# Gated mix of dilated attention and a spatial MLP: the v gathers move to the GpSimd queue, the gate rows move behind the first score gather, and four PSUM banks swap roles

## The chip, the cores and the metric

The kernel runs on one core of a Trainium2 chip. The metric is the device time of one execution in microseconds (us). Four runs of the kernel before the change took 651.54, 651.75, 653.66 and 653.85 us; their median is 652.71 us. The run that was profiled is the one of 653.85 us.

## What is computed

The reference mixes two branches of one input `x` (2048 tokens, 1024 features) with a gate per token:

```python
g = sigmoid((x * gate_w).sum(-1, keepdims=True))
# branch A: attention, 32 heads of 32, each token sees itself and 7 earlier ones, 2 apart
q, k, v = split(x @ wqkv)
idx = pos[:, None] - 2 * arange(8)[None, :]          # masked where negative
o = softmax(q . k[idx] / sqrt(32)) @ v[idx]
a = o @ wo
# branch B: gated MLP over tokens
z = gelu(x @ w_in)                                    # 3584 wide, halves z1 and z2
b = (z1 * (w_sp @ layernorm(z2) + b_sp)) @ w_out
return g * a + (1 - g) * b
```

## The kernel before the change

The matrix products run on TensorE, nearly all of them as Strassen-like quads of seven block products (`strassen`, `chain`), issued by `product` (L402). Each quad owns four PSUM banks. `bank_roles` holds two sets of four banks (banks 0 to 3, banks 4 to 7), and each quad takes one set in the roles X, Y, Z, V and writes back the order in which the next quad takes it (L411 to L413 in `strassen`; the v quads are called with `turn=False` and keep it). Inside a quad VectorE adds the shared product to a bank (`plus`, L473) and ScalarE copies or evacuates banks (L420 to L492, L869). The next block product of the same bank waits for these.

Attention works in eight groups of four heads. For one group g:

- `qk_quad` or `qk_tile` makes q and k.
- `band_blocks` makes three sets of score blocks on banks 4 to 7 (32x64 tiles, L355). ScalarE evacuates each set (L363, 1.8 us for a full one). Two stores per set write it to the DRAM buffer `band_d[g]`. For group 0 there are four such sets (`first_bands`).
- `load_bands` gathers `band_d[g]` into `att_L` by two DMAs, one for each half of the tokens. Each run that they read is `W*HG` = 32 half-precision numbers, 64 bytes.
- VectorE takes maxima and subtracts them (L639 to L642), ScalarE takes the exponential (L630), VectorE makes weights (L651 to L660; L655 multiplies by the gate row `g_att`).
- `load_v` gathers v rows from the DRAM buffer `v_d` into one of two SBUF slots: 128 partitions with a run of `NJJ*C` = 3840 bf16 numbers (7680 bytes) each, 960 KB.
- VectorE multiplies weights and v and adds up (L676, L680, L681, L685; 1.22 us for a product of 2048 columns). Per group this is 18.4 us of VectorE work.

v of groups 0 to 2 is written to `v_d` early, by twelve stores of 128 KB from GpSimd (L310). v of groups 3 to 7 comes later from eight quads (`v_quad`), evacuated by L589 and L595 and stored by SyncE.

The gate is one small product (L995), a tanh (L996), and two scalings into `g_s` and `omg_h` (L997, L998). Two stores write them to the DRAM rows `g_d` and `og_d`; a gather of 8 KB brings `g_d` back as `g_att`, in the layout of attention.

The order of work is written out by a planner inside the kernel. It keeps a clock for TensorE, ScalarE, VectorE, SyncE and the DMA engines. `due` holds transfers with the time from which they may be issued; `advance` issues them, and picks VectorE's attention steps, in the order of their planned times. `settle` pins every instruction of these engines behind the one before it, so that the engines run exactly that order. This begins at `live[0] = True`, just behind the gate. `T_START` sets three planner times at that point: when the score stores of group 0 have landed, when the score banks are free, and when the v stores have landed. GpSimd is not in the planner and not pinned: its instructions run in program order as soon as their semaphores allow.

Every plain DMA from `live[0] = True` on goes through SyncE (shown as L189, a helper line), so it stands in one queue behind all earlier ones. In the order before the change, SyncE issues: the last score stores of group 0, the two gate rows, the two score gathers of group 0, the gather of `g_att`, the v gather of group 0, the v and q/k weights, the v gather of group 1.

While group g = 2 (and g = 4) is worked on, `among_bands` issues the seven products of one quad and puts a score set behind some of them: behind products 1, 3 and 6, but for g = 2 behind 1, 3 and 5. Then the eight v quads follow, the first one alone for two products (X and V), then a pair of marker products on banks 5 and 6 (`mark`, L558), then two quads at a time.

Of the kernel before, what the change touches and what calls it, by code (L numbers as in the profile page):

```python
# [13 lines left out]
P = 128  # L14
S = 2048
# [6 lines left out]
C = HG * DH  # L22
W = 8
NJ = 16
NJJ = NJ + 14
# [33 lines left out]
def kernel(  # L59
# [13 lines left out]
    nc = tc.nc  # L73
# [16 lines left out]
    v_d = dpool.tile([NG, S + 16, C], BF, name="v_d")  # L90
# [3 lines left out]
    g_d = dpool.tile([S], F32, name="g_d")  # L94
    og_d = dpool.tile([S], F16, name="og_d")
# [3 lines left out]
    g_s = sm.tile([16, P], F32, name="g_s")  # L99
# [5 lines left out]
    omg_h = sm.tile([16, P], F16, name="omg_h")  # L105
    g_att = sm.tile([P, NJ], F32, name="g_att")
# [91 lines left out]
    sync = _SyncProxy()  # L198
# [3 lines left out]
    clock = dict(PE=0.0, ACT=0.0, DVE=0.0, SP=0.0, DMA=0.0)  # L202
    live = [False]
    pinned = {}
# [52 lines left out]
    def dma(ready, dur, f, landed=None, timed=False):  # L257
        if not live[0]:
            return f()
        item = [ready, dur, f, landed, timed]  # L260
        due.append(item)
        return item
# [64 lines left out]
    for i in range(4):  # L327
        vp_tile(i, middle=None)
    band_at = [0]
    last_sub = [None]  # L330
    last_evac = [None]
    BAND_SETS = [(0, 8, 2), (1, 1, 7), (9, 1, 7)]

# [1 line left out]
    stored = {}  # L335

    def band_blocks(g, first, step, n, pairs=None):
        qt, kt_ = qT_slots[g % 2], kT_slots[g % 2]
        if first == 0:
            st = band0  # L340
        else:
            st = band_slots[band_at[0] % 3]
            band_at[0] += 1
        for item in stored.get(id(st), ()):
            issue(item)
        ready = pe(T_BAND * (0.3 if n < 3 else 1.0), band_free[0])
        lo = W - 1 if first == 0 else 0
        for m in range(n):
            e, b = divmod(first + m * step, 8) if pairs is None else (m // pairs, first + m % pairs)
            for q in range(2):  # L350
                skip = lo if q == 0 else 0
                at = P * b + QB * q
                for h in range(HG):
                    hp = slice(DH * h, DH * (h + 1))
                    nc.tensor.matmul(banks[4 + h][QB * q:QB * (q + 1), m * KW + skip:(m + 1) * KW], qt[hp, e, at:at + QB],  # L355
                                     kt_[hp, e, at - (W - 1) + skip:at + QB], start=True, stop=True,
                                     tile_position=(DH * h, QB * q), skip_group_check=True)
        band_free[0] = act(0.55 if n < 3 else 1.73, ready + 0.2) + 0.15
        if lo:
            nc.scalar.copy(st[QB:P, 0:n, 0:lo, :], _sub_ap(psum_all[QB:P, :], 4 * 512, [[KW, n], [1, lo], [512, HG]]))  # L360
        dst = st[:, 0:n, lo:KW, :]
        src = _sub_ap(psum_all, 4 * 512 + lo, [[KW, n], [1, KW - lo], [512, HG]])
        nc.scalar.copy(dst, src)  # L363
        bd = band_d[g]

        def landed(t):
            band_data[g] = max(band_data[g], t)

        stored[id(st)] = []
        for q in range(2):  # L370
            for e in range(1 if pairs is None else 2):
                k = n if pairs is None else pairs
                dst = bass.AP(tensor=bd.tensor, offset=bd.offset + (2 * first + 16 * e + q) * BS, ap=[[BR, QB], [2 * step * BS, k], [1, BR]])
                src = st[QB * q:QB * (q + 1), e * k:(e + 1) * k].rearrange("p m k h -> p m (k h)")
                stored[id(st)].append(dma(band_free[0], 0.1 * k, lambda dst=dst, src=src: sync.dma_start(dst, src), landed))

    def band_set(g, x):
        band_blocks(g, *BAND_SETS[x])
# [12 lines left out]
    bank_roles = [banks[0:4], banks[4:8]]  # L391
# [4 lines left out]
    last_store = [None]  # L396
# [170 lines left out]
    def v_quad(i):  # L567
        st = vst_slots[i % 4]
        vs = vq_slots[i % 2]

        def parts(m, a, *bs):
            d = st[:, a, :].rearrange("p (g d h) -> p g d h", g=GR, h=HG)
            full = slice(3 * m, 3 * m + 2)
            at, half, hs = (0, 256, slice(0, 2)) if m == 0 else (64, 0, slice(2, 4))
            yield [d[:, full]] + [b[:, at:at + 256].rearrange("p (g h d) -> p g d h", g=2, h=HG) for b in bs]
            yield [d[:, 2, :, hs]] + [b[:, half:half + 64].rearrange("p (h d) -> p d h", h=2) for b in bs]

        for item in stored.get(id(st), ()):
            issue(item)
        stored[id(st)] = []  # L580

        def store(a):
            dv = bass.AP(tensor=v_d.tensor, offset=v_d.offset + (GP * (S + 16) + 16 + (i + 8 * a) * P) * C, ap=[[C, P], [(S + 16) * C, GR], [1, C]])
            stored[id(st)].append(dma(max(clock["ACT"], clock["DVE"]), 0.92, lambda: sync.dma_start(dv, st[:, a, :].rearrange("p (g c) -> p g c", g=GR)), v_landed))

        def put(m, a, b):
            act(0.85, clock["PE"] + 0.2)
            for dst, src in parts(m, a, b):
                nc.scalar.copy(dst, src)  # L589
            if m:  # L590
                store(a)

        def put_sum(m, a, b):
            dve(0.75, clock["PE"] + 0.2)
            insts = [nc.vector.tensor_tensor(dst, src, v, ALU.add) for dst, src, v in parts(m, a, b, vs)]  # L595
            if not m:
                store(a)
            return insts[0]

        return strassen([wvr[0][:, k, :] for k in K4], [wvr[0][:, 4 + k, :] for k in K4], [wvr[1][:, 4 + k, :] for k in K4],  # L600
                        *[[wvs[q][:, k, :] for k in K4] for q in range(4)], *x_tiles(i), vs,
                        lambda X: put(0, 0, X), lambda Z: put_sum(0, 1, Z), lambda V: put(1, 0, V), lambda Y: put_sum(1, 1, Y),
                        N=VH, flip=True, turn=False)

    def load_v(g):
        v_t = v_slots_t[g % 2]
        sync.dma_start(v_t, bass.AP(tensor=v_d.tensor, offset=v_d.offset + (g * (S + 16) + 2) * C, ap=[[NJ * C, P], [1, NJJ * C]]))


    FR, LATE, WZ_LATE = 0.4, 0.5, 4.0  # L610
# [215 lines left out]
    SQH = 8  # L826
    squares = [(n, x) for n in range(16) for x in range(2)]
    LEAN = (True, True)
    T_START = (0.0, 0.0, 0.0)

    def square(n, x, junk):
        c = slice(x * HF, (x + 1) * HF)
# [48 lines left out]
    BAND_AT = (1, 3, 6)  # L881

    def among_bands(g, quad):
        x = 0
        for n in range(7):
            next(quad)
            step()
            if n + 1 in (BAND_AT if g != 2 else (1, 3, 5)):
                band_set(g, x)
                x += 1  # L890
                step()
        bands_have[0] = g + 1
        next(quad, 0)
# [101 lines left out]
    gate_mm = nc.tensor.matmul(glT, gl_s[:], ident32[:], start=True, stop=True)  # L995
    gate_act = nc.scalar.activation(omg[:], glT, ACT.Tanh, scale=0.5)  # L996
    nc.vector.tensor_scalar(g_s[:], omg[:], 0.5, 0.5, ALU.mult, ALU.add)  # L997
    gate_vec = nc.vector.tensor_scalar(omg_h[:], omg[:], -0.5, 0.5, ALU.mult, ALU.add)  # L998
    sync.dma_start(bass.AP(tensor=g_d.tensor, offset=g_d.offset, ap=[[P, 16], [1, P]]), g_s[:])
    gate_dma = sync.dma_start(bass.AP(tensor=og_d.tensor, offset=og_d.offset, ap=[[P, 16], [1, P]]), omg_h[:])  # L1000

    settle()
    live[0] = True
    for inst in (gate_mm, gate_act, gate_vec, gate_dma):
        pinned[inst.ins.engine] = inst.ins.name
    for x in clock:
        clock[x] = 0.0
    band_data[0], band_free[0], v_data[0] = T_START
    clock["SP"], clock["DMA"] = 0.5, 1.5
    stored.clear()  # L1010
    bands_have[0] = 1
    next_bands()
    dma(0.0, 0.1, lambda: sync.dma_start(g_att[:], bass.AP(tensor=g_d.tensor, offset=g_d.offset, ap=[[NJ, P], [1, NJ]])))
    next_v(1)
    def load_wvr():
        for m in range(2):
# [8 lines left out]
    for g in range(NG):  # L1025
        main = with_quads(g, group_tiles(g))
        if g in (1, 2, 3, 4):
            load_wqk_later(g + 3, clock["PE"])
        hold[0] = g == NG - 1
        paired = play_group(g)  # L1030
        if not paired:
            play(main[0:8 - (not g)])
        if g == 2:
            first = v_quad(0)
            for _ in range(2):
                next(first)
                step()
            mark(bank_roles[1][1:3], VH)
            run(v_quad(1), first, step=step)
            for i in range(2, 8, 2):  # L1040
                run(v_quad(i), v_quad(i + 1), step=step)
            advance(clock["PE"] + 1.0)
            v_have[0] = NG
            next_v()
            load_later(0, clock["PE"] + 4.0, 6.0)
        if not paired:
            play(main[8 - (not g):])
# [559 lines left out]
            load_act(fp // 2 - 1)  # L1607
    out_sums_late()
    traced[0] = len(nc.cur_bb.bb.instructions)
    pinned[gate_dma.ins.engine] = last_store[0].ins.name  # L1610
    for xa in ((1, 1), (0, 1), (0, 0), (1, 0)):
        load_block(1, *xa)
    act_sums(0)
# [46 lines left out]
```

## Time and profile before

| What | Value |
|---|---|
| Median of four runs | 652.71 us (651.54 to 653.85) |
| The profiled execution | 653.85 us, its span from first to last instruction 652.1 us |
| TensorE (PE) busy | 638.5 us, 98% |
| VectorE (DVE) busy | 519.5 us, 80% |
| ScalarE (ACT) busy | 297.3 us, 46% |
| GpSimd (POOL) busy | 15.4 us, 27 instructions |
| Granted TensorE clock | 1.00 |
| The SyncE queue (q1) | 95.70 MB, 61.6% of the time of 16 DMA engines |
| The GpSimd queue (q0) | 1.57 MB, 0.9% |
| A v gather, 960 KB (8 of them, SyncE) | median 6.8 us from issue to landing |
| A score gather, 64 KB (16) | median 3.4 us |
| A full score store, 248.5 KB (28) | median 4.7 us |
| A v store from GpSimd, 128 KB (12) | median 4.3 us; 0.75 us of GpSimd each |
| The gate rows, 8 KB and 4 KB; `g_att`, 8 KB | 2.7, 2.5 and 2.7 us |

How to read the views: every row of a timeline is a start in us from the first instruction, a length, the engine, the line of the code, the operation, what it writes and reads, and a count. A bracket at the end tells how long the engine stood idle before it, and what ended that wait. SPq rows are DMA issues; the transfer itself follows. In a table of stretches the last two columns are the busy share of the DMA engines and what they moved.

### The profile page before, as it was taken

Reading aid. Unit: us, or ns where it says so; the run is one execution under the profiler, and the core shown is the slowest. Engines: PE = TensorE matmul, PEld = TensorE weight load, DVE = VectorE, ACT = ScalarE, POOL = GpSimd, SP = SyncE. Lnnn points to the kernel's source line nnn. Section 1 sums busy time; section 2 is a strip of 40 time slices with the busy share of each in tenths; the row PEclk is TensorE's granted clock in tenths of the full one; section 3 lists DMA queues with packets and bytes.
Section 4 is the critical chain, followed back from the end, with each engine's and each line's share of the span. In section 5 each row is a group of like instructions: output and inputs, shape, how many; then the busy total and the mean of one; then the engine's idle time right before and its main releaser. Section 6 shows DMA issues by size and latency. Waiting matters only on the chain.

```text
span 652.1 us, 11298 instructions
## 1 busy us (share of the span) xinstructions
PE 638.5 (98%) x4345; PEld 336.7 (52%) x4391; DVE 519.5 (80%) x816; ACT 297.3 (46%) x644; POOL 15.4 (2%) x27
## 2 busy tenths in 40 slices
PE   8999999999989999999999999999999999999997
PEld 4544467444445555444444444444444444868684
DVE  0357988998799999999988766987659999696852
ACT  3557677676667777799644112111121112202120
POOL 2210000000000000001000000000000000000000
PEclk9999999999999999999999999999999999999999
DMA  9979564787778103248985567569587385655411
GB/s 205 193 179 278 119 145 109 171 211 178 160 182 218 22 11 115 64 130 219 267 224 193 120 163 176 125 178 276 114 188 169 93 148 96 121 138 126 117 34 48
DMA packets 227173, 98.18 MB, mean 151 GB/s; under 512 B 174496, under 2 KB 214064, under 8 KB 227120
## 3 DMA queue, kind: packets, MB, share of 16 engines
q1 hardware_dynamic: 226256, 95.70, 61.6%
q0 software_dynamic: 576, 1.57, 0.9%
q8 instruction: 34, 0.56, 0.4%
q14 instruction: 19, 0.16, 0.1%
q10 hardware_dynamic: 288, 0.20, 0.1%
HBM read 44.31 MB, written 36.61 MB: 124 GB/s over the span
## 4 chain that ended last, share of the span: by engine, by line
PE 85%; DVE 4%; ACT 4%; DMA 3%; SPq 2%; issue 1%; DVEq 0%
PE psum_all L402 69%; PE psum_all L1484 8%; PE psum_all L293 4%; DMA band_d<-arena 2%; PE psum_all L303 2%; ACT arena L838 1%; PE psum_all L355 1%; SPq L189 1%; DVE arena L676 1%; ACT arena L1175 1%; DVE psum_all L473 1%; DVE arena L680 1%; DMA arena<-in_A_wqkv_dram 1%; SPq L178 1%; DVE arena L545 0%
## 5 line engine op out<-in xcount | busy, mean ns | idle before, releaser
L402 PE MATMUL psum_all<-arena 128*128 128x512 f16 (+6 forms) x2481 | 502.8, 362 | 6.2 <-DVE psum_all L473 2.7
L402 PEld LDWEIGHTS <-arena 128*128 128x128 f16 (+1 forms) x2518 | 245.1, 98 | 256.4 <-issue 6.6
L676 DVE TENSOR_TENSOR arena<-arena,att_A 128x2048 f16<-128x2048 bf16 x64 | 75.4, 1219 | 0.3
L473 DVE TENSOR_TENSOR psum_all<-psum_all,arena 128x512 f32<-128x512 f32 (+1 forms) x78 | 51.0, 669 | 8.1 <-PE psum_all L402 5.0
L1484 PE MATMUL psum_all<-arena 128*128 128x256 f16 (+1 forms) x468 | 51.7, 273 | 0.0
L1484 PEld LDWEIGHTS <-arena 128*128 128x128 f16 x468 | 45.8, 98 | 5.7
L783 ACT ACTIVATE arena<-psum_all 128x448 bf16<-128x448 f32 x64 | 34.2, 545 | 20.8 <-DVE psum_all L473 10.1
L293 PE MATMUL psum_all<-arena 128*128 128x512 bf16 x183 | 42.0, 379 | 1.3 <-issue 0.6
L420 ACT COPY psum_all<-psum_all 128x512 f32<-128x512 f32 (+1 forms) x24 | 12.5, 520 | 66.1 <-PE psum_all L402 65.4
L1175 ACT ACTIVATE arena<-psum_all 128x512 bf16<-128x512 f32 x56 | 31.2, 615 | 20.8 <-PE psum_all L402 12.9
L680 DVE TENSOR_TENSOR arena<-arena 128x2048 f16<-128x2048 f16 x32 | 37.9, 1217 | 0.0
L363 ACT CAST arena<-psum_all 128x1988 f16<-128x1988 f32 (+3 forms) x25 | 34.0, 1359 | 2.8 <-PE psum_all L355 2.3
L838 ACT ACTIVATE arena<-arena 128x896 bf16<-128x896 bf16 x32 | 30.9, 980 | 0.0
L545 DVE TENSOR_TENSOR arena<-arena 128x512 f16<-128x512 bf16 (+5 forms) x60 | 30.1, 534 | 0.4
L444 ACT COPY psum_all<-psum_all 128x512 f32<-128x512 f32 (+1 forms) x24 | 12.3, 518 | 37.5 <-PE psum_all L402 36.8
L293 PEld LDWEIGHTS <-arena 128*128 128x128 bf16 x192 | 18.1, 98 | 21.6 <-DMA arena<-in_A_wqkv_dram 0.7
L869 ACT CAST arena<-psum_all 128x512 bf16<-128x512 f32 x40 | 22.2, 591 | 12.2 <-DVE psum_all L473 9.9
L388 DVE TENSOR_TENSOR arena<-arena 128x2048 f16<-128x2048 bf16 x8 | 9.4, 1221 | 22.2 <-ACT gl_s L306 21.0
L426 ACT COPY arena<-psum_all 128x512 f32<-128x512 f32 (+1 forms) x24 | 12.7, 533 | 26.4 <-PE psum_all L402 23.3
L486 ACT COPY psum_all<-psum_all 128x512 f32<-128x512 f32 (+1 forms) x39 | 21.7, 574 | 6.1 <-PE psum_all L402 5.5
L431 ACT COPY psum_all<-psum_all 128x512 f32<-128x512 f32 (+1 forms) x24 | 12.4, 516 | 25.6 <-PE psum_all L402 24.8
L549 DVE TENSOR_TENSOR arena<-arena 128x1024 f16<-128x1024 f16 (+1 forms) x16 | 11.3, 713 | 15.7 <-PE psum_all L402 15.7
(113 smaller groups left out, 531.2 us busy)
## 6 DMA issues: line engine op xcount, KB each, us to landing
arena<-v_d SPq DMA_DIRECT2D x8, 960.0 KB, 6.8
z_d<-arena SPq DMA_DIRECT2D x14, 512.0 KB, 3.8
arena<-z_d SPq DMA_DIRECT2D x14, 512.0 KB, 4.3
zg_d<-arena SPq DMA_DIRECT2D x56, 128.0 KB, 2.2
arena<-zg_d SPq DMA_DIRECT2D x32, 224.0 KB, 3.5
band_d<-arena SPq DMA_DIRECT2D x28, 248.5 KB, 4.7
arena<-in_A_wqkv_dram SPq DMA_DIRECT2D x16, 256.0 KB, 4.5
o_d<-arena SPq DMA_DIRECT2D x4, 1024.0 KB, 6.2
```

The costliest lines, as they stand in the source:

```text
L293: nc.tensor.matmul(ps[:], w[:, t, kt, :], xT[:, kt, 512 * c:512 * (c + 1)], start=(kt == 0), stop=(kt == KT - 1))
L363: nc.scalar.copy(dst, src)
L402: nc.tensor.matmul(bank[:, 0:N], lhsT, rhs, start=(start and m == 0), stop=(m == n - 1), skip_group_check=True)
L473: last_add[0] = nc.vector.tensor_tensor(out[:, n], a[:, n], vs, ALU.add)
L545: return [lambda a=a: nc.vector.tensor_tensor(*a) for a in args]
L676: lambda ws=ws, in0=in0, in1=in1: tt(p5[:, ws], in0[:, ws], in1[:, ws], ALU.mult)), False
L680: lambda a=p3[:, ws], b=p3[:, ws.start + 4:ws.stop + 4]: tt(a, a, b, ALU.add)), not n
L783: nc.scalar.activation(z2[:, i + 8 * a, ZC * c:ZC * (c + 1)], bank[:, 0:ZC], ACT.Gelu_apprx_tanh, accum_out=s1[:, 4 * n + c:4 * n + c + 1])
L838: return nc.scalar.activation(junk, src, ACT.Square, accum_out=(s2, s2h)[x][:, n:n + 1])
L869: nc.scalar.copy((qT_slots, kT_slots)[t][g % 2][:, :, 256 * (c + 2 * x):256 * (c + 2 * x + 1)], bank[:].rearrange("p (n e) -> p e n", e=2))
L1175: last_gelu[0] = nc.scalar.activation(z1s[:, f, a, :], bank[:], ACT.Gelu_apprx_tanh)
L1484: nc.tensor.matmul(bank[:, h], l, r, start=(start and m == 0), stop=(m == len(ab) - 1), skip_group_check=True)
```

## The change

Three edits, and the planner times that go with them:

- `load_v` issues its gather from GpSimd instead of SyncE. The planner still counts it as a SyncE transfer. The v time in `T_START` goes from 0.0 to 3.0.
- The two gate rows are no longer stored before the pinned part begins. They become planned transfers behind `load_bands(0)`, followed by the gather of `g_att`. SyncE is pinned from the last score store of group 0 on (`last_band`) instead of from the gate stores, and the planner's SyncE and DMA clocks start earlier.
- For g = 2 the score sets come behind products 1, 3 and 6 as for g = 4. Ahead of the v quads the first set of banks is reordered: X and Z stay, Y and V change places.

```diff
+        last_band[0] = stored[id(st)][-1]
...
     def load_v(g):
         v_t = v_slots_t[g % 2]
-        sync.dma_start(v_t, bass.AP(tensor=v_d.tensor, offset=v_d.offset + (g * (S + 16) + 2) * C, ap=[[NJ * C, P], [1, NJJ * C]]))
+        nc.gpsimd.dma_start(v_t, bass.AP(tensor=v_d.tensor, offset=v_d.offset + (g * (S + 16) + 2) * C, ap=[[NJ * C, P], [1, NJJ * C]]))
...
-    T_START = (0.0, 0.0, 0.0)
+    T_START = (-1.0, 0.0, 3.0)
...
-            if n + 1 in (BAND_AT if g != 2 else (1, 3, 5)):
+            if n + 1 in BAND_AT:
...
-    sync.dma_start(bass.AP(tensor=g_d.tensor, offset=g_d.offset, ap=[[P, 16], [1, P]]), g_s[:])
-    gate_dma = sync.dma_start(bass.AP(tensor=og_d.tensor, offset=og_d.offset, ap=[[P, 16], [1, P]]), omg_h[:])
...
-    for inst in (gate_mm, gate_act, gate_vec, gate_dma):
+    for inst in (gate_mm, gate_act, gate_vec, last_band[0]):
...
-    clock["SP"], clock["DMA"] = 0.5, 1.5
+    clock["SP"], clock["DMA"] = -0.5, 0.0
...
     next_bands()
-    dma(0.0, 0.1, lambda: sync.dma_start(g_att[:], bass.AP(tensor=g_d.tensor, offset=g_d.offset, ap=[[NJ, P], [1, NJ]])))
+    dma(0.6, 0.1, lambda: sync.dma_start(bass.AP(tensor=g_d.tensor, offset=g_d.offset, ap=[[P, 16], [1, P]]), g_s[:]))
+    dma(0.6, 0.1, lambda: sync.dma_start(bass.AP(tensor=og_d.tensor, offset=og_d.offset, ap=[[P, 16], [1, P]]), omg_h[:]))
+    dma(0.6, 0.1, lambda: sync.dma_start(g_att[:], bass.AP(tensor=g_d.tensor, offset=g_d.offset, ap=[[NJ, P], [1, NJ]])))
...
         if g == 2:
+            r = bank_roles[0]
+            bank_roles[0] = [r[0], r[3], r[2], r[1]]
             first = v_quad(0)
```

More of the change, by code (lines that the diff above doesn't have):

```diff
@@ L329 @@
     band_at = [0]
-    last_sub = [None]
+    last_band = [None]
     last_evac = [None]
@@ L1609 @@
     traced[0] = len(nc.cur_bb.bb.instructions)
-    pinned[gate_dma.ins.engine] = last_store[0].ins.name
+    pinned[last_store[0].ins.engine] = last_store[0].ins.name
     for xa in ((1, 1), (0, 1), (0, 0), (1, 0)):
```

## The prediction

> **What bounds the kernel.** The first part of the page: TensorE is busy 638.5 of 652.1 us at a clock of 1.00. A change that leaves the products alone can only gain where TensorE stands still. So I read TensorE's waits first, and then the timeline around each of the long ones.
>
> ```profile
> PE 638.5 (98%) x4345; PEld 336.7 (52%) x4391; DVE 519.5 (80%) x816; ACT 297.3 (46%) x644; POOL 15.4 (2%) x27
> ...
> PE psum_all L402 <- DVE psum_all L473: 2.7, 2, 2.1
> ...
> PE psum_all L355 <- ACT arena L363: 1.1, 2, 0.9
> ...
> PE psum_all L402 <- ACT arena L869: 0.4, 1, 0.4
> ```
>
> The columns of the waits are total, count and longest. These three rows hold 4.2 us, and all of it lies between 52 and 193 us. The timeline there has three places.
>
> ```profile
> 43.77 2.23 POOL L310 DMA_DIRECT2D v_d<-arena  x3 [10.65 <-ACT gl_s L306]
> ...
> 47.88 1.29 SPq L189 DMA_DIRECT2D att_L<-band_d  x2
> ...
> 50.04 0.35 SPq L189 DMA_DIRECT2D arena<-v_d  x1
> ...
> 51.80 0.29 DVE L639 TENSOR_TENSOR att_m<-att_L 128x256 f16<-128x256 f16 x1 [2.94 <-DMA att_L<-band_d]
> ...
> 52.96 0.69 DVE L473 TENSOR_TENSOR psum_all<-psum_all,arena 128x512 f32<-128x512 f32 x1
> ...
> 53.71 3.70 PE L402 MATMUL psum_all<-arena 128*128 128x512 f16 x15 [0.63 <-DVE psum_all L473]
> ```
>
> First place: VectorE is in order. It waits 2.94 us for the first score gather, and the L473 behind the maxima is what TensorE then waits 0.63 us for. Whatever the gather loses, TensorE loses one for one.
>
> ```profile
> 82.26 0.64 PE L355 MATMUL psum_all<-arena 32*64 32x71 bf16 x56 [0.16 <-ACT arena L363]
> ...
> 85.71 0.70 PE L402 MATMUL psum_all<-arena 128*128 128x320 f16 x4 [0.43 <-ACT arena L869]
> ```
>
> Second place: the third score set of g = 2 waits 0.16 us for the evacuation of the second, and the V product of the first v quad waits 0.43 us for a bank.
>
> ```profile
> 157.06 0.59 SPq L189 DMA_DIRECT2D arena<-v_d  x1
> ...
> 172.21 0.29 DVE L639 TENSOR_TENSOR att_m<-att_L 128x256 f16<-128x256 f16 x1 [3.54 <-DMA att_L<-band_d]
> ...
> 179.75 0.27 PE L355 MATMUL psum_all<-arena 32*64 32x64 bf16 x16 [0.92 <-ACT arena L363]
> ...
> 191.68 1.16 DVE L473 TENSOR_TENSOR psum_all<-psum_all,arena 128x448 f32<-128x448 f32 x2
> ...
> 192.36 7.84 PE L402 MATMUL psum_all<-arena 128*128 128x448 f16 x39 [2.10 <-DVE psum_all L473]
> ```
>
> Third place: the v gather of group 4 enters SyncE's queue at 157.06 and lands 6.5 us later. Score stores issued behind it at 157.70, 162.22 and 162.85 take 8.0, 6.3 and 6.7 us (median of their kind 4.7). So the score gather of group 5 comes late and VectorE waits 3.54 us. From 172.21 to 193 it never idles again, and carries the delay to the L473 of 191.68: 2.10 us of TensorE. The same wait holds ScalarE's exponential and the evacuations behind it: 0.92 us.
>
> **The change, part by part.**
>
> **Gate rows: 0.** Their two issues (0.35 and 0.37 us, at 46.08 and 46.52) leave their place ahead of the gather. But the queue is free from 46.89 and the gather goes at 47.88: by the chain, when the score store of 43.82 lands. So nothing is gained; at most 0.7 us, if that landing were not the later one. Put behind, they make SyncE wait for the landing of `g_d` (2.7 us) ahead of `g_att` and of the v and q/k weights, which start some 2.3 us later than at 50.44. `g_att` would land near 55 instead of 51.9; L655 reads it at 56.21. The v weights take 7.7 us and are read at 60.16, so 1.5 us are spare, and the 960 KB of v ahead of them in that queue are gone. If this cover failed it would cost up to 0.8 us.
>
> **First two v gathers: +3.5 us.** GpSimd has nothing else to do, so a gather there starts when its semaphores allow. The v stores of groups 0 and 1 (43.77 and 44.52) land after 3.9 and 3.8 us, at 47.7 and 48.3. With 0.75 us of GpSimd each, as a v store takes, the gathers issue at 47.7 and 48.5 instead of 50.04 and 57.05. That is right beside the score gather (issued 47.88 and 48.55, landed 51.7), which before had the DMA engines to itself:
>
> ```profile
> 48.00:49.00 1.00, 1.00 (x6) 0.39 (x4) 0.86 (x2) 0.43 (x1) 0.00 (x0) 1.00 0.00 1
> 49.00:50.00 1.00, 1.00 (x6) 0.48 (x5) 0.00 (x0) 0.99 (x3) 0.00 (x0) 1.00 0.66 63
> 50.00:51.00 1.00, 1.00 (x7) 0.42 (x5) 0.00 (x0) 0.67 (x2) 0.00 (x0) 1.00 0.59 56
> ...
> 52.00:53.00 1.00, 1.00 (x5) 0.39 (x4) 0.90 (x5) 0.00 (x0) 0.00 (x0) 1.00 1.01 392
> ```
>
> The last two columns are DMA share and GB/s: small score runs move at about 60 GB/s, the v gather at 392. At that rate 960 KB take 2.5 us. How much of it passes ahead of the score runs the trace does not show directly. Ends: 0 (the queues do not disturb each other) and 5.0 us (both v gathers first). Nearest row: the three GpSimd stores of 128 KB (1.0 us at 392 GB/s). Score stores issued at 41.8 to 42.6 land in 2.2 to 2.4 us; those of 43.17 and 44.48, beside them, need 4.2 and 3.6. They lost 1.2 to 2 us, no less than the whole GpSimd transfer. So I take all of the first gather (2.5) and, as the second starts 0.8 us later, some 1.0 of it. TensorE then waits 4.1 us instead of 0.63.
>
> [...]
>
> [...]
>
> **Banks: -0.5 us.** Behind product 6 the third score set finds its banks free (0.16 gone), and V is now the bank evacuated two products earlier (0.43 gone). What is late next: Y now waits for the second last evacuation, and the markers on banks 5 and 6 for the L363 of the set that moved one product (0.86 us) back; it ended at 85.17 against markers at 86.25, so about 0.1 returns. Ends: 0 and -0.6.
>
> **Later v gathers: -1.0 us.** The gather of group 4 goes from 157.06 to 146.4, when its slot is last read. The stores of 157.7 to 162.9 lose 2.5 us of transfer ahead of them. But at 148 to 151 it now passes the third score store of group 4 (148.54), whose gather VectorE already waits 1.44 us for at 156.61. That makes VectorE up to 2.5 us later there: free at 171.2 instead of 168.66, while the group 5 scores land near 170.4 instead of 172.1. VectorE is 1.0 us earlier at 191.68, and TensorE with it. Ends: -3.2 (0.92, 2.10 and 0.15 at 195 all go) and +0.5 (the gather of group 5, at 179, delays the group 6 scores). Group 2's goes from 94.56 to 85.6 beside score stores; that may hold VectorE 1.3 us at 94.5, which its idle 0.81 and 0.72 us before L595 at 106 and 114 take up: 0, and 1.3 if not.
>
> **Sum.** 0 + 3.5 - 0.5 - 1.0 = +2.0 us on the profiled 653.85 (span 652.1, 1.75 around it). That run is 1.14 us above the median of the four, so I state the time from the median: 652.7 + 2.0 = 654.7.
>
> **Rivals.**
>
> - **The gain is the whole of the waits (faster).** One mechanism: the score runs keep their pace beside v. For it: with v in SyncE's own queue, everything behind waited, and that goes. Against: the 3.6 and 4.2 us above. Then 0 - 0.5 - 2.5: 649.7. It decides from a first score gather that lands before 52.2.
> - **Both gathers pass first.** The score gather lands 5 us late, near 56.7, and group 5's gather gives back the later gain: +5.0 - 0.5 + 0.5: 657.7. For it: the rows above allow it; against: the second gather starts late.
> - **It moves transfers that are hidden anyway.** The delay stays under 1.5 us and cancels with the banks and the later gain: 652.7. For it: 98% busy TensorE.
>
> **How the numbers follow.** Forecast (+1.0 to +3.0): 0.42; all waits go: 0.28; both pass first: 0.20; cancels: 0.10. A measurement of this kernel can tell 0.3%, 2.0 us, from no change. Six tenths of the forecast's chance lie beyond it. Slower: 0.20 + 0.25 = 0.45; same: 0.10 + 0.17 = 0.27; faster 0.28. The range takes in both far cases: 649.3 to 657.7.
>
> **What would show it.** GpSimd issues near 47.7 and 48.5 with the DMA share near 1 from 49 on; the wait ahead of L639 grows from 2.94 to about 6.4 and TensorE's from 0.63 to about 4.1; no waits of 0.16 and 0.43 at 82 and 86; the waits of 0.92 and 2.10 shrink by 1 in all. I am wrong if L639 starts near 51.8 as before, if the planner's shifted times put the L473 ahead of the maxima, or if a new wait stands ahead of `g_att` or the v weights.

## The result, and the profile after

The changed kernel takes 655.88 us (median of 34 runs, 652.8 to 664.7), the kernel before 652.72 us (55 runs beside them, 651.1 to 655.9). The ratio is 1.0056, with a 95% interval of 1.004 to 1.0071: some 3.7 us slower. The ratio leaves out runs that lie 1.5% above the fastest as disturbed; that drops 7 of the 34 here and 2 of the 12 in e12_after_again below, although the experiments show that such long runs belong to the change.

The 34 runs form two groups: 22 from 652.8 to 657.7 us (median 655.5), and 12 from 661.3 to 664.7 us (median 663.5). The kernel before has only one. The profiled run, 655.03 us with a span of 652.9, is of the lower group. From its page, the engines and the GpSimd queue (packets, MB, share):

```profile
PE 639.9 (98%) x4346; PEld 336.9 (52%) x4391; DVE 519.5 (80%) x816; ACT 297.7 (46%) x644; POOL 19.7 (3%) x35
...
q0 software_dynamic: 1728, 9.44, 4.9%
```

GpSimd has eight instructions more, and its queue 7.9 MB more. TensorE is busy 1.4 us longer with the same products, though nothing was added to it. TensorE's waits (total, count, longest):

```profile
PE psum_all L403 <- DVE psum_all L474: 2.7, 1, 2.7
...
PE psum_all L355 <- ACT arena L363: 0.6, 1, 0.6
PE psum_all L559 <- ACT arena L363: 0.4, 1, 0.4
```

Lines behind the edit stand one further down (L402 is now L403, L473 is L474, L639 is L640). Of the three waits on products, the first (0.63 at 53 us) is gone, the last has grown from 2.10 to 2.65, and the marker has a new one. The timeline at the first and the third place:

```profile
44.01 2.23 POOL L310 DMA_DIRECT2D v_d<-arena  x3 [10.65 <-ACT gl_s L306]
...
45.18 1.57 SPq L189 DMA_DIRECT2D att_L<-band_d  x2
...
47.76 1.10 POOL L608 DMA_DIRECT2D arena<-v_d  x2 [1.51 <-DMA v_d<-arena]
...
49.42 0.29 DVE L640 TENSOR_TENSOR att_m<-att_L 128x256 f16<-128x256 f16 x1 [0.32 <-DMA att_L<-band_d]
...
146.41 0.53 POOL L608 DMA_DIRECT2D arena<-v_d  x1 [23.91 <-DVE arena L652]
...
146.77 1.26 SPq L189 DMA_DIRECT2D band_d<-arena  x2
...
148.19 7.36 SPq L189 DMA_DIRECT2D att_L<-band_d  x2
...
158.77 0.29 DVE L640 TENSOR_TENSOR att_m<-att_L 128x256 f16<-128x256 f16 x1 [3.91 <-DMA att_L<-band_d]
...
171.15 0.29 DVE L640 TENSOR_TENSOR att_m<-att_L 128x256 f16<-128x256 f16 x1 [0.33 <-DMA att_L<-band_d]
...
179.08 0.53 POOL L608 DMA_DIRECT2D arena<-v_d  x1 [32.15 <-DVE arena L677]
...
185.13 0.29 DVE L640 TENSOR_TENSOR att_m<-att_L 128x256 f16<-128x256 f16 x1 [0.92 <-DMA att_L<-band_d]
...
192.31 7.90 PE L403 MATMUL psum_all<-arena 128*128 128x448 f16 x32 [2.65 <-DVE psum_all L474]
```

In this run the first score gather was issued at 45.18 and 45.91, 2.7 us earlier than in the profile of before, and landed at 48.6 and 49.3, before much of v was moving. So L640 starts at 49.42 and not near 55. At the third place VectorE now waits 3.91 us for the scores of group 4 (1.44 before), 0.33 for those of group 5 (3.54 before) and 0.92 for those of group 6 (none before). The scores of group 4 are late because their last two stores, issued at 146.77 and 147.40 just behind the v gather of 146.41, take 7.2 and 7.5 us (3.7 and 4.7 before). So the second half of their gather goes at 155.00 (153.97 before), and it takes 3.7 us (2.5 before). VectorE comes to its L474 at 191.63, and before it was 191.68. Behind that wait TensorE's clock falls. A table of stretches, whose third column from the end is the granted clock:

```profile
50.00:51.00 1.00, 1.00 (x7) 0.41 (x6) 0.62 (x2) 0.67 (x2) 0.00 (x0) 1.00 0.97 369
...
190.00:193.00 3.00, 0.69 (x4) 0.39 (x4) 2.97 (x6) 1.26 (x5) 0.00 (x0) 1.00 0.95 246
...
194.00:197.00 3.00, 3.00 (x9) 1.22 (x8) 3.00 (x4) 1.38 (x5) 0.00 (x0) 0.52 0.86 193
```

The first row shows v moving at 369 GB/s from 50 us on. The last shows half speed behind the idle stretch at 190 to 193: this is the extra busy time of TensorE. The kernel before has no such stretch in its profile (mean clock 1.000).

### The profile page after: what moved, and what is told of

It is laid out like the page before. It is cut to its first block, busy times and chain, and to the rows that moved or that the text cites. A ratio compares the mean times of both kernels' runs of the same rounds, so it can differ in the third digit from the quotient of the medians.

```text
span 652.9 us, 11311 instructions
## 1 busy us (share of the span) xinstructions
PE 639.9 (98%) x4346; PEld 336.9 (52%) x4391; DVE 519.5 (80%) x816; ACT 297.7 (46%) x644; POOL 19.7 (3%) x35
## 4 chain that ended last, share of the span: by engine, by line
PE 82%; DMA 6%; ACT 4%; DVE 3%; SPq 3%; issue 2%; DVEq 0%; ACTq 0%
PE psum_all L403 70%; PE psum_all L1487 8%; DMA band_d<-arena 3%; PE psum_all L303 2%; DMA att_L<-band_d 2%; PE psum_all L293 2%; ACT arena L839 1%; SPq L178 1%; DVE arena L677 1%; ACT arena L1178 1%; DMA arena<-in_A_x_dram 1%; PE psum_all L355 1%; SPq L189 1%; DVE arena L546 1%; ACT arena L784 0%
## 5 line engine op out<-in xcount | busy, mean ns | idle before, releaser
L403 PE MATMUL psum_all<-arena 128*128 128x512 f16 (+6 forms) x2482 | 504.5, 362 | 5.6 <-DVE psum_all L474 2.7
L403 PEld LDWEIGHTS <-arena 128*128 128x128 f16 (+1 forms) x2518 | 245.6, 98 | 256.9 <-issue 7.9
L474 DVE TENSOR_TENSOR psum_all<-psum_all,arena 128x512 f32<-128x512 f32 (+1 forms) x78 | 51.0, 669 | 10.6 <-PE psum_all L403 7.4
L546 DVE TENSOR_TENSOR arena<-arena 128x512 f16<-128x512 bf16 (+5 forms) x60 | 30.1, 534 | 0.3
L303 PE MATMUL psum_all<-arena 128*128 128x385 bf16 x128 | 22.7, 330 | 1.2 <-DMA arena<-in_A_x_dram 0.9
```

The costliest lines, as they stand in the source:

```text
L303: nc.tensor.matmul(ps[:, 0:VP + 1], xT[:, kt, i * P:(i + 1) * P], wvp[:, kt, :], start=(kt == 0), stop=(kt == KT - 1))
L403: nc.tensor.matmul(bank[:, 0:N], lhsT, rhs, start=(start and m == 0), stop=(m == n - 1), skip_group_check=True)
L474: last_add[0] = nc.vector.tensor_tensor(out[:, n], a[:, n], vs, ALU.add)
L546: return [lambda a=a: nc.vector.tensor_tensor(*a) for a in args]
```

## Experiments

All are small edits of one of the two kernels, timed beside runs of the kernel before. They ran in three sets, each on a chip of its own, with a median of the kernel before of 652.81, 651.37 and 652.60 us; so across sets compare ratios rather than times. "Clock" says whether the profile shows half speed behind a wait. First and third place are TensorE's longest waits near 53 and 192 us.

| Kernel | Median (range), us | Before, us | Ratio, 95% interval | First / third place, us | Clock |
|---|---|---|---|---|---|
| e1_v_alone | 664.13 (661.1 to 664.9) | 652.81 | 1.0160, 1.0139 to 1.0182 | 5.23 / 2.65 | half at 58 |
| e3_v01_only | 659.46 (659.0 to 661.3) | 652.81 | 1.0103, 1.0085 to 1.0121 | 5.32 / 1.63 | half at 58 |
| e2_v01_sync | 655.34 (654.9 to 656.6) | 652.81 | 1.0039, 1.0024 to 1.0054 | 0.31 / 3.16 | half at 194 |
| e6_no_v | 653.03 (651.4 to 655.6) | 652.81 | 1.0002, 0.9987 to 1.0018 | 0 / 1.10 | full |
| e7_v01_behind | 656.50 (653.0 to 659.6) | 651.37 | 1.0064, 1.0041 to 1.0087 | 0 / 2.97 | half at 194 |
| e8_all_behind | 653.79 (651.8 to 657.3) | 651.37 | 1.0030, 1.0014 to 1.0047 | 0 / 0.46 | full |
| e9_v4_only | 653.48 (652.2 to 657.1) | 651.37 | 1.0031, 1.0014 to 1.0047 | 0 / 2.09 | full |
| e10_v5_only | 652.78 (651.2 to 655.5) | 651.37 | 1.0015, 1.0000 to 1.0031 | 0 / 1.62 | full |
| e12_after_again | 655.89 (653.9 to 664.5) | 652.60 | 1.0040, 1.0022 to 1.0058 | 4.99 / 3.47 | half at 56 and 200 |
| e4_gate | 653.17 (651.7 to 655.5) | 652.60 | 1.0007, 0.9991 to 1.0023 | 0 / 1.03 | full |
| e5_banks | 652.24 (651.0 to 654.9) | 652.60 | 0.9989, 0.9974 to 1.0004 | 0 / 0.07 | full |
| e11_v45_behind | 652.86 (651.0 to 654.4) | 652.60 | 1.0001, 0.9982 to 1.0019 | 0 / 0.35 | full |

The theory: score runs of 64 bytes and score stores starve beside a v gather from GpSimd. The rivals: A, the gate rows; B, the banks and the planner's order; C to F stand in the expectations below.

### The v gathers alone, in two halves, and not at all

e1_v_alone is the kernel before with one line changed:

```diff
-        sync.dma_start(v_t, ...
+        nc.gpsimd.dma_start(v_t, ...
```

> The kernel before, with only the eight v gathers issued from GpSimd; gate rows, banks and planner times as before. Theory (v pieces starve the small score runs on the DMA engines): as slow as the changed kernel or slower, median 655 to 657 us, with a third of the runs above 660, because the first score gather here still goes behind the gate rows (issue near 47.9 us) and so beside the v gathers of 47.7 and 48.5. Rival A (gate rows moved behind the gather, and the round trip of the gate row that then holds SyncE): 650 to 652.7, no run above 657. Rival B (banks and the order that the planner makes of them): the same 650 to 652.7.

All five runs lie above 661, more than the theory had given. Its last score store of group 0 landed early (45.0), but the gate rows held the score gather back to 46.80 and 47.48. The second half then entered at the same time as the first v gather (47.55) and took until 56.12. Rivals A and B fall: neither is in this kernel.

The next three start from the changed kernel. The order of the instructions on TensorE, VectorE and ScalarE is the same in all of them as in it.

```diff
+        (sync if g < 2 else nc.gpsimd).dma_start(v_t, ...      # e2_v01_sync
+        (nc.gpsimd if g < 2 else sync).dma_start(v_t, ...      # e3_v01_only
+        sync.dma_start(v_t, ...                                # e6_no_v
```

> The changed kernel, with the v gathers of groups 0 and 1 back on SyncE; those of groups 2 to 7 stay on GpSimd. Theory: the runs of 661 to 665 us, a third of the changed kernel's, are the first score gather caught beside the two v gathers; they are gone, all runs lie between 652 and 657. What the later gathers cost stays: the V products of the third place (192 us) still wait 2 us or more for VectorE, median 653.5 to 655. Rivals A (gate rows) and B (banks, planner): the spread of the changed kernel stays, a third above 660.

> The changed kernel, with only the v gathers of groups 0 and 1 on GpSimd; those of groups 2 to 7 back on SyncE. Theory: some runs above 660 us stay, near a third; the others are about 1 us quicker than the changed kernel's (652 to 654), with the waits of the third place as before the change (0.9 and 2.1 us). Rival C (the later gathers make the slow runs): no run above 657, median 652 to 653.

> The changed kernel with all eight v gathers back on SyncE: gate rows behind the first score gather and the banks changed, nothing else. Theory: the gate rows and banks are worth 0 to -1 us, so 651.5 to 652.7 and no run above 657. Rivals A and B: 655 to 656, with runs above 660 as in the changed kernel.

e6 is level with before: the loss is in the v gathers. e2, without the first two, has no run above 656.6; what is left of the loss is 2.3 us against e6. Its third place, in the timeline:

```profile
159.69 0.29 DVE L640 TENSOR_TENSOR att_m<-att_L 128x256 f16<-128x256 f16 x1 [4.07 <-DMA att_L<-band_d]
...
193.73 6.57 PE L403 MATMUL psum_all<-arena 128*128 128x448 f16 x25 [3.16 <-DVE psum_all L474]
```

and the same place in e6, where the v gather stands in SyncE's queue behind the scores of group 4:

```profile
154.79 0.29 DVE L640 TENSOR_TENSOR att_m<-att_L 128x256 f16<-128x256 f16 x1
155.22 0.59 SPq L189 DMA_DIRECT2D arena<-v_d  x1
...
190.77 9.55 PE L403 MATMUL psum_all<-arena 128*128 128x448 f16 x48 [1.10 <-DVE psum_all L474]
```

VectorE gets the scores of group 4 without a wait in e6, and after 4.07 us in e2. e3 missed its expectation in a telling way: not a third but all five of its runs are long, so by the times its first gather was caught every time (the one profile shows it). Rival C falls too.

### Which of the later gathers

Only that of group 4, or only that of group 5, is on GpSimd:

```diff
+        (nc.gpsimd if g == 4 else sync).dma_start(v_t, ...     # e9_v4_only
+        (nc.gpsimd if g == 5 else sync).dma_start(v_t, ...     # e10_v5_only
```

> The changed kernel with only the v gather of group 4 on GpSimd (issued near 147 us, beside the score stores and the gather of group 4). Theory: that score gather lands some 3 us later than with the gather on SyncE (near 158 instead of 155), VectorE stays late to the end, and the third place waits 2 to 3 us: 653.8 to 655.3, most of the 2.3 us that the later gathers cost together. Rival E (the gather of group 5 beside the score gather of group 6 is what costs): 652.5 to 653.3.

> The changed kernel with only the v gather of group 5 on GpSimd (issued near 180 us, beside the second half of the score gather of group 6). Theory: VectorE waits about 1 us more at 186, the third place about 2 us: 653 to 654. Rival E: 654.5 to 655.5.

The waits came near what the theory said: 3.64 us for the scores of group 4 in e9 (its score gather landed at 158.2) and 2.09 at the third place; in e10 0.89 for those of group 6 and 1.62 at the third place, where about 2 was expected. The medians lie just below the theory's ranges, which were reckoned from a before of 652.8; the before beside these runs is 651.4. Against that e9 costs 2.1 us and e10 1.4. The two intervals overlap widely, so that group 4 is the dearer one is likely and not shown. Rival E, by which the gather of group 5 is what costs, had e10 as the slower of the two; the order came out the other way, and the wait in e9 needs no help of group 5. No kernel with all gathers on SyncE and the other two edits ran in this set; that those edits cost nothing is taken over from e6. Both profiles are at full clock. Over all its runs, 5 of e9's 12 and 3 of e10's 12 have a mean clock below 0.9985, and of the 32 of before beside them one has.

### The gathers stay on GpSimd, but wait for the scores

The first of these kernels makes the v gathers of groups 0 and 1 wait for the landing of the first score gather. The second makes every v gather wait for the last score gather ahead of it in the program. The third does so for groups 4 and 5 only, and has the rest on SyncE.

```diff
+            gathered[0] = sync.dma_start(L[:, 256 * e:256 * e + 256]...
...
+        inst = nc.gpsimd.dma_start(v_t, ...
+        if g < 2:                                # e7; e8 always, e11 for g in (4, 5)
+            tc.add_manual_dep(inst.ins, gathered[0].ins.name, SYNC, ...)
```

> The changed kernel; the v gathers of groups 0 and 1 stay on GpSimd, but wait for the landing of the first score gather. Nothing else moves. Theory (the v transfer beside the score runs is what costs): no run above 659 us, the first wait of TensorE (53 us) below 0.7 us, median as with these two gathers on SyncE, 654.5 to 656. Rival D (issuing a v gather from GpSimd costs wherever it stands, say by what it does to VectorE or to the queue): 657 to 661, TensorE's first wait above 2 us.

> The changed kernel with all eight v gathers on GpSimd, each waiting for the landing of the last score gather that stands ahead of it in the program (that of group 0 for v of 0 and 1, of 2 for 2 and 3, of 4 for 4, of 6 for 5, of 7 for 6 and 7). Theory: the collisions of groups 4 and 6 go as well, the third place (192 us) waits 1.5 us or less and keeps its full clock: 651.5 to 653.3 us. Rival D: 654.5 to 657, with the third place at 2.5 us or more.

> The changed kernel with only the v gathers of groups 4 and 5 on GpSimd, each behind the landing of the score gather of group 4 and 6; the other six on SyncE. Theory: SyncE's queue is free of them and no score transfer is beside them, so the third place waits 0.5 to 1.1 us at full clock and nothing is late near 60: a ratio to before of 0.997 to 0.999. Rival D (the gathers cost on GpSimd wherever they stand): 1.001 to 1.003.

The waits came out as the theory said: no first wait in e7, and a third place of 0.46 us in e8 and 0.35 in e11, at full clock. The times did not: e7 and e8 are 0.5 us above the theory's ranges (1.9 us, reckoned from the before of 651.4 beside them), e11 0.9 us. In e8 the timeline shows one reason:

```profile
63.46 2.75 PE L403 MATMUL psum_all<-arena 128*128 128x512 f16 x11 [0.75 <-DVE psum_all L474]
...
191.00 9.17 PE L403 MATMUL psum_all<-arena 128*128 128x448 f16 x46 [0.46 <-DVE psum_all L474]
```

The 0.75 us at 63.46 is new: the delayed v gathers (49.31 and 49.86) now run beside the v weights, and VectorE's L546 waits 1.45 us for these at 61.1. In e7 the two waits are 0.70 and 1.39 us. The second reason is time outside the span, told at the end. One run of e7 (659.6) is above what was expected; its cause is open. Between e7 and e8, which differ only in groups 2 to 7, lie 2.7 us, near the 2.3 between e2 and e6. Rival D gave e7 a first wait above 2 us and e8 a third place of 2.5 us, and falls on both. Its times do not fall: reckoned from the before of 651.4, e7 and e8 lie inside its ranges. So that gathers on GpSimd cost something even where they meet no scores is left of it: e8 is 2.4 us above before, the two reasons come to 1.2 of these, and the rest is open. e11 has neither reason:

```profile
180.70 0.55 POOL L608 DMA_DIRECT2D arena<-v_d  x1 [25.11 <-DMA att_L<-band_d]
...
189.81 10.49 PE L403 MATMUL psum_all<-arena 128*128 128x448 f16 x53 [0.35 <-DVE psum_all L474]
```

Its span is, with that of e5, the shortest of all profiles (649.2 us). Still its median is that of before, where 0.997 to 0.999 was expected: no version here beats the kernel before. Why the short third place does not show in the medians is open; the profile of before is of a run 1.1 us above its median, and e5 shows 0.07 us at that place with v in its old queue.

### Gate rows alone, banks alone

> The kernel before with the gate rows alone moved behind the first score gather, SyncE pinned from the last score store and the planner's start times changed with it; v gathers on SyncE, banks as before. The prediction's step says 0, at most -0.7: a ratio to before of 0.999 to 1.000. Rival F (the move costs, since SyncE waits for the landing of the gate row): 1.001 to 1.002, with a new wait of TensorE for the v weights near 60.

> The kernel before with the bank roles and the places of the score sets of g = 2 alone changed. The prediction's step says -0.5 us, a ratio of 0.999; the traces of the changed kernel say 0, since the waits of 0.16 and 0.43 us at 82 and 86 are replaced by 0.36 (marker behind the score evacuation, 85) and 0.2 to 0.5 (bank, 88).

The gate rows alone are worth nothing that these runs can tell (1.0007). The interval does not exclude the 1.001 to 1.002 of rival F, but its sign is missing: the profile of e4 has no new wait for the v weights near 60. The banks alone give 0.9989, with 1 inside the interval. In the profile of e5 the waits of 0.16 and 0.43 us are replaced by 0.12 at the marker and 0.49 at 88 us, the same 0.6; what else moved in its favour is within what runs differ.

### The changed kernel once more

> The changed kernel as it is, beside the others on one chip. Theory (whether the last score store of group 0 gets out ahead of GpSimd's v stores, near 43.8 us, decides): two clusters of times, 653 to 657 and 661 to 665. If the profile falls in the upper one, the second half of the first score gather lands near 56, TensorE waits about 5 us at 53 and runs at half its clock for 3 us behind; in the lower one that wait is below 0.7 us and the third place waits 2.5 us or more. Rival (the long runs have another cause, without a place): a long run whose profile shows the first gather on time.

Two of the 12 runs are long, and the profile fell on one of them (664.45 us):

```profile
44.20 2.23 POOL L310 DMA_DIRECT2D v_d<-arena  x3 [10.64 <-ACT gl_s L306]
...
47.69 1.28 SPq L189 DMA_DIRECT2D att_L<-band_d  x2
...
48.35 1.10 POOL L608 DMA_DIRECT2D arena<-v_d  x2 [1.92 <-DMA v_d<-arena]
...
56.58 0.29 DVE L640 TENSOR_TENSOR att_m<-att_L 128x256 f16<-128x256 f16 x1 [7.31 <-DMA att_L<-band_d]
...
58.48 2.29 PE L403 MATMUL psum_all<-arena 128*128 128x512 f16 x5 [4.99 <-DVE psum_all L474]
```

The gather is issued at 47.69 and 48.43, as late as in the profile of before. Its first half lands after 2.9 us, its second, which entered 0.08 us behind the first v gather, after 8.1 us. The clock, in stretches:

```profile
52.00:56.00 4.00, 1.49 (x7) 0.58 (x6) 0.00 (x0) 0.38 (x1) 0.00 (x0) 1.00 0.91 318
56.00:60.00 4.00, 1.52 (x4) 0.55 (x4) 2.49 (x8) 1.10 (x2) 0.00 (x0) 0.50 0.45 95
60.00:64.00 4.00, 3.78 (x12) 1.42 (x11) 3.55 (x7) 1.76 (x3) 0.00 (x0) 0.65 1.18 331
```

So the long runs are the first gather caught beside v: 5.0 us of waiting, about 2.2 us for the products from 58.5 to 62.8 at half clock, and a third place that is dearer than in the profile of the lower group: 3.47 us of waiting, with a clock of 0.84 in the stretch from 198 to 200 and of 0.50 from 200 to 202.

What decides which group a run falls in is in the traces as well: the lead of the last score store of group 0 over GpSimd's first v store.

| Profile | Lead, us | The store lands after, us |
|---|---|---|
| e9, e8, e1, e7, after | 1.20, 1.12, 1.03, 1.00, 0.79 | 2.1 to 2.4 |
| e6, e11, e5, e4, e10 | 0.37, 0.27, 0.17, 0.06, 0.05 | 3.6 to 4.2 |
| e12, e3, before | -0.11, -0.28, -0.71 | 3.6 to 4.0 |

With a lead of 0.8 us the store is through before v, and the gather that waits for it goes near 45. Without it the store itself takes 3.6 to 4.2 us beside GpSimd's stores, and the second half of the gather goes after 47, into the v gathers. This is read from 13 profiles; the lead itself was not forced by an experiment. It changes from run to run; why e3 was late in all five runs, and the changed kernel in 14 of 46, was not found.

## Why the prediction was right and wrong, point by point

The forecast of +2.0 us was right in direction and near in size (+3.2 between the medians, just above the +1.0 to +3.0 of the forecast), but its terms were not; errors of both signs cancelled, so the nearness is luck.

- **Gate rows: 0.** Right alone (e4). Wrong as a term of this sum: with v on GpSimd their place decides whether the gather gets away in time. With the rows ahead of it (and the old banks, which matter little by e5) the kernel takes 664.1 us (e1), with the rows behind it 655.9. The failed step is "nothing is gained; at most 0.7 us": an edit was priced without the other edit of the same change.
- **First two v gathers: +3.5.** The mechanism was right, the size was never 3.5. In the profiles TensorE's first wait is 0 or near the upper end: 0 in the profiled run, 4.99, 5.23 and 5.32 us in e12, e1 and e3. The bound of 5.0 from 960 KB twice at 392 GB/s was good; the value from the nearest row (1.2 to 2 us lost beside three stores) was not. The failed step is the fixed start: I took the gather's 47.88 from one profile, while in these profiles it starts anywhere from 43.9 to 47.7, by a lead of half a microsecond more or less. In e12 the half of the gather that was issued behind the first v gather took 8.1 us, the half issued 0.66 us ahead of it 2.9; the tiny `g_att` gather took 2.7 us before and 6.4 us beside v (after). How the two queues share the DMA engines is in no view.
- **Banks: -0.5.** Not found. The failed step is "about 0.1 returns": the waits at 85 and 88 us (0.36 and 0.23) return all of the 0.59. In the profile after:

```profile
85.55 0.43 PE L559 MATMUL psum_all<-arena 128*128 128x320 bf16 x2 [0.36 <-ACT arena L363]
...
88.40 1.79 PE L403 MATMUL psum_all<-arena 128*128 128x320 f16 x12 [0.23 <-ACT psum_all L421]
```

- **Later v gathers: -1.0.** Wrong in sign: e2 lies 2.3 us above e6. Group 4's wait grew by 2.47 us, the 2.5 that I gave as its most, and group 5's shrank by 3.21. But the scores of group 4 made VectorE 2.16 us late at 158.77, and the gather of group 5 beside the scores of group 6, which stood in the prediction only as the upper end of +0.5, added 0.92. VectorE arrived 0.05 us earlier, not 1.0. TensorE, without its earlier waits, was there 0.6 us sooner, and so waited longer. The 0.92 us near 180 did not hang on the wait for group 5 as the prediction has it: 0.61 us stands there with that wait at 0.33 us (after) and at 3.60 us (e3).
- **What the sum did not hold.** Half clock behind the waits: of the 35 runs recorded with the result, 28 have a mean clock below 0.9985 (all 12 long ones and 16 of the other 23); of the 35 runs of the kernel before beside e12, 3 have. A stretch of 3.4 us at 0.5 costs 1.7 us, and among those 23 runs the 16 have a median of 655.6 us, the other 7 of 654.0. And 0.4 us lies outside the span. These two make some 2.0 us of the 2.75 by which the lower group is above before. The longer third wait adds nothing to them, since TensorE came to it 0.60 us sooner: it ends at 192.31, and before at 192.36. The other 0.7 us is open; the profile of before is of a run 1.1 us above its median, so the two profiles cannot settle it.
- **Rivals.** "Both gathers pass first" (657.7) is what happens in the long runs, at a price 6 us higher, since the clock and the third place were left out. "It moves transfers that are hidden anyway" (652.7) falls by the interval of the ratio, 1.004 to 1.0071. "The gain is the whole of the waits" came true at the first place only, and not because the score runs keep their pace beside v: in the lower group, by its one profile, they were gone before v came.

## What to carry to other kernels

Before a large transfer moves to a second queue, list the small transfers that will be under way beside it, because a v gather of 960 KB that met 64-byte runs held them for microseconds here (8.1 us in e12, where the half issued ahead of v took 2.9). Making it wait for those on the path took the long waits away here (first place 0, third 0.46 us in e8 and 0.35 in e11), but gained nothing over the one queue: 1.0030 with all eight gathers (e8), 1.0001 with two (e11). A start time from one profile is a sample: if two engines come within a microsecond of each other, price both orders. To a wait of TensorE like the 2.65 us and more of these runs add a possible stretch at half clock (3.4 us at 0.5 in the profile after).

## What the runs showed of the hardware beyond that

- **Issuing beside VectorE.** The issues of v gathers took 0.53 to 0.56 us of GpSimd each in all these profiles, less than the 0.75 us assumed. In the profile after, VectorE was busy for 4.0 of the 4.3 us of the eight issues.
- **The clock and the length of a wait.** Half speed (a clock of 0.50 to 0.62 over 2 us) followed waits of 2.65 (after), 2.97 (e7), 3.16 (e2) and 3.47 us (e12), and none of 2.10 (before), 2.09 (e9) and 1.63 us (e3). But the 2.65 us at the third place of e1 were followed by full speed (1.00 from 196 to 202 us): length alone does not decide. What else does was not shown.
- **Time outside the span.** With 0, 1 or 2 of the v gathers on GpSimd, a run is 1.77 to 1.80 us longer than its span (mean of each kernel's runs), as for the kernel before; with 6 (e2) it is 1.96, with 8 it is 2.18 to 2.19 (after, e7, e8, e12), and 2.33 in e1. The ranges of 0 to 2, of 6 and of 8 do not overlap. So 0.4 us of the change is in no line of the profile; what it is stays open.
